# Attention without a row maximum, keys on partitions, under an order written by hand

## The chip, the cores and the metric

The kernel runs on one NeuronCore of one Trainium2 chip. The metric is the time of one execution on the device in microseconds; lower is better. The kernel before was timed three times: median 2095.51 us, from 2094.62 to 2095.75 us. All arithmetic is in float32.

## The reference, cut to what matters

Eight batches, twelve heads, 448 tokens and 64 dimensions a head; q and k are normalised by their root mean square over d, then softmax attention, and the result, 3584 rows of 768, goes through two matrix products with g = h - tanh(h) between them.

```python
q_n, k_n = (rmsnorm(q, g_q), rmsnorm(k, g_k))      # x / rms * g
scale = 1.0 / np.sqrt(q.shape[-1])
scores = scale * np.matmul(q_n, k_n.transpose(0, 1, 3, 2))
scores = scores - np.max(scores, axis=-1, keepdims=True)
attn = np.exp(scores)
attn = attn / (np.sum(attn, axis=-1, keepdims=True) + 1e-09)
attn_out = np.matmul(attn, v)                       # (8, 12, 448, 64) -> x: (3584, 768)
h = x @ w_in                                        # w_in: 768 x 2048
out = (h - np.tanh(h)) @ w_out                      # w_out: 2048 x 768
```

The inputs come from a fixed seed. g_q and g_k are |normal| + 0.5 in 64 entries each; drawn as the reference draws them, the largest product of the two is 5.26. The two weights reach the kernel as float64.

## The kernel before, in words

The work is 48 steps of attention, one for each batch and pair of heads, and eight batches of the two-layer MLP. 448 tokens lie on 112 partitions, four to a partition, so every token tile is a chunk c of 112.

`load` (L75) brings k, q and v of a step in, three DMAs on the queue of SyncE (SP). `prep` (L155) does the norm: GpSimd (POOL) squares 112x512 elements (L162), VectorE (DVE) sums them (L164) and adds the mean's terms (L165), POOL raises to the power -0.5 (L168), DVE multiplies (L169); four transposes on TensorE (PE, L176) turn the result so that (head, d) lies on partitions, and it is copied out of PSUM, for k with g_q * g_k * scale (L179), for q by ScalarE (ACT, L183). This happens for k and for q apart.

`attention` (L188) then takes each of four query chunks and two heads: a matmul gives scores with queries on partitions and keys free (L199), DVE finds the negated maximum of each row (L202), ACT does exp with that as its bias and sums the row on the way (L206), DVE turns the sum into a reciprocal (L210, L214), ACT multiplies the row by it (L215). Because the product with v has to contract over keys, every 112x112 block is transposed on PE (L223, 32 a step) and copied out of PSUM by DVE (L229) or ACT (L231); then the matmuls with v run (L233), two heads in the two halves of one PSUM tile. One copy puts the result into `xT` (L238), with tokens in their natural order.

`mlp_h` (L244) makes 128 hidden units of a batch: six matmuls of 448 columns (L252), tanh on ACT (L257), two subtractions on DVE (L260). `mlp_out` (L262) makes 128 tokens by 384 outputs: 16 matmuls (L268), an eviction (L274, L276), a store. In the trace every float32 matmul counts as two MATMUL instructions, a transpose as one.

`load_weight` (L113) turns a piece of a weight from the two words of each float64 into float32: four DVE instructions (L134, L141, L144, L147), three on POOL (L135, L138, L151) and one on ACT (L150), on 128x768 elements, 32 pieces in all. The loads go through ACT's queue (L124, L127).

The program text puts the attention of batch 0 with all weight pieces first, and then, for every batch, the attention of the next batch between its MLP units. What runs when on each engine isn't as written: the framework's scheduler orders the instructions by priority and by its own estimates of time, and picks free buffers. PSUM is split in three tiles for scores, two for transposes, one for the product with v and two for the MLP.

Of the kernel before, what the change touches and what calls it, by code (L numbers as in the profile page):

```python
# [9 lines left out]
F32 = mybir.dt.float32  # L10
I32 = mybir.dt.int32
U32 = mybir.dt.uint32
# [6 lines left out]
@with_exitstack  # L19
def kernel(  # L20
    ctx: ExitStack,
    tc: tile.TileContext,
    q: bass.AP,
    k: bass.AP,
    v: bass.AP,
    g_q: bass.AP,
    g_k: bass.AP,
    moe_w_in: bass.AP,
    moe_w_out: bass.AP,
    out: bass.AP,  # L30
):
    """Attention on pairs of heads, all in float32, one batch ahead of the MLP.

    Tokens of a batch lie on partitions as token = NCH * p + c, so that a load reads
    NCH whole rows per partition. A pair of heads gives 128 rows of x transposed,
    (head, d) on partitions and tokens free, which is what the MLP contracts over.
    """
# [3 lines left out]
    NT, DM = out.shape  # L41
    DFF = moe_w_out.shape[0]
    P = 128
    NCH = 4
# [7 lines left out]
    scale = 1.0 / float(D) ** 0.5  # L52
    assert 2 * D == P and NP == CD and 2 * REST == P and B % 2 == 0

    consts = ctx.enter_context(tc.tile_pool(name="consts", bufs=1))
# [30 lines left out]

    gcol = consts.tile([P, 2], F32, name="gcol")
    for base in (0, D):
        nc.scalar.dma_start(out=gcol[base : base + D, 0:1], in_=g_q[:, None])
        nc.scalar.dma_start(out=gcol[base : base + D, 1:2], in_=g_k[:, None])  # L90
    g_col = consts.tile([P, 1], F32, name="g_col")
    nc.vector.tensor_scalar(
        out=g_col, in0=gcol[:, 0:1], scalar1=gcol[:, 1:2], scalar2=scale, op0=ALU.mult, op1=ALU.mult
    )
    ident = consts.tile([P, P], F32, name="ident")
    make_identity(nc, ident)
    neg_half = consts.tile([CP, 2 * NCH], F32, name="neg_half")
    nc.vector.memset(neg_half, -0.5)

# [5 lines left out]
    w_in_words, w_out_words = (  # L105
        bass.AP(
            tensor=dataclasses.replace(w.tensor, shape=[w.shape[0], 2 * w.shape[1]], dtype=I32),
            offset=0, ap=[[2 * w.shape[1], w.shape[0]], [1, 2 * w.shape[1]]],
        )
        for w in (moe_w_in, moe_w_out)  # L110
    )

    def load_weight(pool, n):  # L113
        """A 128-wide piece of a weight, from the two words of its float64 to float32, rounded to nearest.

        2^20 + the upper mantissa bits + lo * 2^-32 is rounded once, to the float32 mantissa. Its power of
        two is the exponent field moved to float32's bias: 0 below its normal range, infinity above it.
        """
        f = n % CF
        raw = pool.tile([P, CD, P, 2], I32, name="w_raw")  # L120
        if n < CF:
            dst = w_in_sb[f].rearrange("p c f -> p (c f)")
            src = w_in_words[:, f * 2 * P : (f + 1) * 2 * P].rearrange("(c p) f -> p c f", p=P)
            nc.scalar.dma_start(out=raw.rearrange("p c f w -> p c (f w)"), in_=src)  # L124
        else:
            dst = w_out_sb[f]
            nc.scalar.dma_start(  # L127
                out=raw.rearrange("p c f w -> p (c f w)"), in_=w_out_words[f * P : (f + 1) * P, :]
            )
        lo, hi = (raw.rearrange("p c f w -> p (c f) w")[:, :, i] for i in range(2))  # L130
        ex = pool.tile([P, DM], I32, name="w_exp")
        man = pool.tile([P, DM], I32, name="w_man")
        exf, manf = ex.bitcast(F32), man.bitcast(F32)
# [208 lines left out]
```

## Time and profile before

| | value |
|---|---|
| median of three runs | 2095.51 us |
| span of the profiled execution | 2092.5 us |
| PE busy | 1931.4 us (92%), 6784 matmul instructions |
| DVE busy | 824.6 us (39%), 2142 instructions |
| ACT busy | 701.6 us (34%), 1581 instructions |
| POOL busy | 398.3 us (19%), 294 instructions |
| moved by DMA | 70.44 MB |

The profiled execution is known by its span, from its first instruction to its last; it lies 3.0 us under the median of the runs, which is what comes before and after the span. Busy time of PE is not PE at its best rate, because matmuls overlap and their ends are modelled. A row of the groups gives the line, the engine, what is written from what, the shape, the count, then the busy time in us, the mean of one in ns, the idle time of the engine ahead of it and who ended that. A row of the chain of waits gives a start, a duration and the work in it.

### The profile page before, as it was taken

How to read it: one execution, taken by the hardware profiler on the slowest of the kernel's cores; microseconds unless marked ns; L12 is line 12 of the kernel's file. 1: busy time of each engine (PE TensorE's matmuls, PEld its weight loads, DVE VectorE, ACT ScalarE, POOL GpSimd, SP SyncE). 2: the span in 40 equal slices, each digit the busy share in tenths (PEclk: the TensorE clock that was granted, in tenths of full speed). 3: DMA queues.
4: the chain of work that ended last, by engine and by line, in shares of the span. 5: the costliest groups of instructions: out<-in, count | busy, mean ns of one | idle time of the engine just before them, and what ended most of it. 6: DMA issues, size and time to landing. Idle time of an engine off the chain costs nothing. (4 is left out here: it accounts for less than half of the span.)

```text
span 2092.5 us, 19112 instructions
## 1 busy us (share of the span) xinstructions
PE 1931.4 (92%) x6784; PEld 938.5 (45%) x6784; DVE 824.6 (39%) x2142; ACT 701.6 (34%) x1581; POOL 398.3 (19%) x294
## 2 busy tenths in 40 slices
PE   4767689999999999999999999999999999999999
PEld 1322234454444544445444544445444554445555
DVE  6877764412543044432435025531455025430100
ACT  3344354412543034522445025530454024440100
POOL 5667642101221011111212012210122012100000
PEclk9766699999999999999999999999999999999999
DMA  4433310000000000000000000000000000000000
GB/s 113 128 104 127 119 42 27 19 25 25 22 23 26 19 21 27 22 26 24 22 23 23 24 25 23 27 22 19 27 23 27 20 24 18 5 2 22 0 12 19
DMA packets 58015, 70.44 MB, mean 34 GB/s; under 512 B 4160, under 2 KB 55872, under 8 KB 57920
## 3 DMA queue, kind: packets, MB, share of 16 engines
q1 hardware_dynamic: 42752, 44.05, 7.0%
q10 hardware_dynamic: 15168, 25.17, 3.8%
q8 instruction: 54, 0.88, 0.2%
q14 instruction: 41, 0.34, 0.0%
HBM read 58.20 MB, written 11.01 MB: 33 GB/s over the span
## 5 line engine op out<-in xcount | busy, mean ns | idle before, releaser
L252 PE MATMUL mm<-xT,w_in 128*128 128x448 f32 x1536 | 649.6, 549 | 1.9 <-DVE xT L238 1.9
L268 PE MATMUL mm<-w_out,gT 128*128 128x384 f32 x1536 | 504.9, 488 | 0.0
L268 PEld LDWEIGHTS mm<-w_out,gT 128*128 128x128 f32 x1536 | 289.0, 191 | 200.1 <-issue 9.9
L252 PEld LDWEIGHTS mm<-xT,w_in 128*128 128x128 f32 x1536 | 270.0, 195 | 210.4 <-issue 204.5
L223 PE MATMUL tp<-ident,attn 112*112 112x112 f32 x1536 | 254.0, 282 | 99.8 <-ACT attn L215 93.2
L223 PEld LDWEIGHTS tp<-ident,attn 112*112 112x112 f32 x1536 | 167.2, 138 | 372.0 <-ACT attn L215 229.8
L199 PE MATMUL sc<-kT,qT 64*112 64x448 f32 x768 | 284.7, 619 | 15.4 <-ACT attn L206 11.7
L162 POOL TENSOR_TENSOR n<-k_nat 112x512 f32<-112x512 f32 x48 | 52.4, 1091 | 1186.8 <-issue 1170.8
L215 ACT ACTIVATE attn<-attn,rden 112x448 f32<-112x448 f32 x384 | 238.6, 660 | 92.4 <-DVE rden L214 54.8
L206 ACT ACTIVATE attn<-sc,nmax 112x448 f32<-112x448 f32 x384 | 237.9, 623 | 81.7 <-DVE nmax L202 81.6
L233 PE MATMUL av<-attnT,v_nat 112*64 112x448 f32 x768 | 222.8, 586 | 13.7 <-DVE attnT L229 13.4
L202 DVE TENSOR_REDUCE nmax<-sc 112x1 f32<-112x448 f32 x384 | 225.1, 614 | 4.0 <-PE sc L199 2.6
L276 DVE COPY o_sb<-mm 128x384 f32<-128x384 f32 x28 | 15.6, 558 | 530.2 <-PE mm L268 530.2
L229 DVE COPY attnT<-tp 112x448 f32<-112x448 f32 x192 | 119.8, 624 | 257.8 <-PE tp L223 253.8
L231 ACT COPY attnT<-tp 112x448 f32<-112x448 f32 x192 | 101.9, 531 | 298.4 <-PE tp L223 284.4
L257 ACT ACTIVATE th<-mm 128x448 f32<-128x448 f32 x128 | 68.8, 538 | 300.6 <-PE mm L252 300.5
L274 ACT COPY o_sb<-mm 128x384 f32<-128x384 f32 x28 | 13.4, 480 | 463.6 <-PE mm L268 463.6
L199 PEld LDWEIGHTS sc<-kT,qT 64*112 64x112 f32 x768 | 93.9, 183 | 148.2 <-ACT attn L206 112.7
L260 DVE TENSOR_TENSOR gT<-mm,th 128x384 f32<-128x384 f32 x128 | 70.7, 553 | 150.2 <-ACT th L257 149.9
L233 PEld LDWEIGHTS av<-attnT,v_nat 112*64 112x64 f32 x768 | 49.0, 139 | 133.6 <-DVE attnT L229 103.8
L168 POOL TENSOR_TENSOR rr_q<-rr_q,neg_half 112x8 f32<-112x8 f32 x48 | 80.0, 1668 | 79.0 <-DVE rr_q L165 78.8
L168 POOL TENSOR_TENSOR rr_k<-rr_k,neg_half 112x8 f32<-112x8 f32 x48 | 80.9, 1684 | 66.6 <-DVE rr_k L165 66.1
(36 smaller groups left out, 1034.5 us busy)
## 6 DMA issues: line engine op xcount, KB each, us to landing
w_raw<-in_moe_w_in_dram ACTq DMA_DIRECT2D x16, 768.0 KB, 4.8
w_raw<-in_moe_w_out_dram ACTq DMA_DIRECT2D x16, 768.0 KB, 4.3
k_nat<-in_k_dram SPq DMA_DIRECT2D x48, 224.0 KB, 2.6
q_nat<-in_q_dram SPq DMA_DIRECT2D x48, 224.0 KB, 2.6
v_nat<-in_v_dram SPq DMA_DIRECT2D x48, 224.0 KB, 2.6
out_dram<-o_sb SPq DMA_DIRECT2D x48, 192.0 KB, 1.9
out_dram<-o_sb SPq DMA_DIRECT2D x16, 96.0 KB, 2.2
gcol<-in_g_q_dram ACTq DMA_DIRECT2D x2, 0.2 KB, 3.4
```

What stands on the lines that cost most here:

```text
L168: nc.gpsimd.tensor_tensor(out=rr, in0=rr, in1=neg_half, op=ALU.pow)
L199: nc.tensor.matmul(sc[:CP, :S], lhsT=qT[r, c * CP : (c + 1) * CP], rhs=kT[r, :], start=True, stop=True)
L202: nc.vector.tensor_reduce(out=nmax[:, h, c : c + 1], in_=sc[:CP, :S], op=ALU.max, axis=AX.X, negate=True)
L206: nc.scalar.activation(a, sc[:CP, :S], AF.Exp, bias=nmax[:, h, c : c + 1], scale=1.0, accum_out=den[:, h, c : c + 1],)
L215: nc.scalar.mul(a, a, rden[:, h, c : c + 1])
L223: nc.tensor.transpose(tp[:CP, c * CP : (c + 1) * CP], attn[h, c][:, kc * CP : (kc + 1) * CP], ident[:CP, :CP],)
L229: nc.vector.tensor_copy(out=aT[h], in_=tp[:CP, :S])
L231: nc.scalar.copy(out=aT[h], in_=tp[:CP, :S])
L233: nc.tensor.matmul(av[h * D : (h + 1) * D, :S], lhsT=v_nat[:, h, kc, :], rhs=aT[h], start=(kc == 0), stop=(kc == NCH - 1),)
L252: nc.tensor.matmul(hps[:, :S], lhsT=w_in_sb[f][:, c, :], rhs=xT[b, c], start=(c == 0), stop=(c == CD - 1),)
L260: nc.vector.tensor_tensor(out=dst, in0=hps[:, a:z], in1=th[:, a:z], op=ALU.subtract)
L268: nc.tensor.matmul(ops[:, :HALF], lhsT=g[:, f, :], rhs=w_out_sb[f][:, d], start=(f == 0), stop=(f == CF - 1),)
```

## The change

The kernel now has two paths and picks one at run time. It multiplies g_q and g_k, takes the largest square, compares it with (60 / (scale * 64))^2 = 7.5^2, reads the flag into a register, and branches. Where the flag is set, scores can't pass 60 in size and `bounded_path` runs; else `general_path`, which is the kernel before.

In `bounded_path`:

- The scores are made with keys on partitions and queries free, so that exp gives the operand for the product with v directly. The row maximum, the multiplication of each row and the 32 transposes of a step with their copies go. The 1e-9 goes too.
- k is turned without its norm; the norm of a key is the scale of exp, one value for each partition. One power instruction serves q and k together.
- The sum over keys is a matmul with a matrix of ones, of 64 columns for each head, beside the product with v. From batch 1 on, DVE first adds the four chunks of keys (`add`); in batch 0 the ones are multiplied with all four chunks. DVE takes the reciprocal of the 128x448 sums and multiplies the product with v by it.
- MLP: one subtraction of 448 columns in place of two; POOL copies the last 64 tokens for the shared tile.
- Weights are rounded in 64 half pieces. All loads, weights included, go through SP's queue.
- The order on each engine is the order of the program text (`manual_schedule`). `slot(s)` holds the work of attention for four neighbouring steps; between its parts stand four gaps, each of which issues a quarter of a slot's MLP matmuls, from slot 6 on. The 32 half pieces of w_in are spread over the gaps of slots -2 to 5, one a gap; those of w_out over the gaps of slots 6 to 8.

```diff
+    def norm(s):
+        rr = small.tile([CP, 2, 2 * NCH], F32, name="rr", bufs=3)
+        for i, name in enumerate("kq"):
+            rows = loaded[name, s].rearrange("p a b d -> p (a b) d")
+            sq = nat.tile([CP, 2 * NCH, D], F32, name="n", bufs=1)
+            nc.gpsimd.tensor_tensor(out=sq, in0=rows, in1=rows, op=ALU.mult)
+            nc.vector.reduce_sum(rr[:, i], sq, axis=AX.X)
+        rr2 = rr.rearrange("p i r -> p (i r)")
...
+        nc.gpsimd.tensor_tensor(out=rr2, in0=rr2, in1=neg_half, op=ALU.pow)
...
+    def scores(s, half):
+        rr, kT, qT = turned[s]
+        p = probs[s, half] = pp.tile([CP, 2, NCH // 2, S], F32, name="p")
+        for i in range(NCH // 2):
+            c = half * (NCH // 2) + i
+            tiles = []
+            for h in range(2):
+                r = slice(h * D, (h + 1) * D)
+                sc = ps_s.tile([P, 512], F32, name="sc")
+                nc.tensor.matmul(
+                    sc[:CP, :S], lhsT=kT[r, c * CP : (c + 1) * CP], rhs=qT[r, :], start=True, stop=True
+                )
+                tiles.append(sc)
+            for h in range(2):
+                nc.scalar.activation(
+                    p[:, h, i, :], tiles[h][:CP, :S], AF.Exp, scale=rr[:, 0, 2 * c + h : 2 * c + h + 1]
+                )
+
+    def add(s):
+        if s < NP:
+            sums[s] = []
+            return
+        t = sp.tile([CP, 2, S], F32, name="sum")
+        sums[s] = [t]
+        for h in range(2):
+            a, z = (probs[s, half][:, h].rearrange("p c q -> p (c q)") for half in range(2))
+            u = sp.tile([CP, 2 * S], F32, name="sum2")
+            nc.vector.tensor_tensor(out=u, in0=a, in1=z, op=ALU.add)
+            nc.vector.tensor_tensor(out=t[:, h, :], in0=u[:, :S], in1=u[:, S:], op=ALU.add)
+
+    def values(s):
...
+        for c in range(NCH):
+            p = probs[s, c // 2]
+            for h in range(2):
+                nc.tensor.matmul(
+                    av[h * D : (h + 1) * D, :S], lhsT=v_nat[:, h, c, :], rhs=p[:, h, c % 2, :],
+                    start=(c == 0), stop=(c == NCH - 1),
+                )
+        dn = ps_v.tile([P, 512], F32, name="dn")
+        t = sums.pop(s)
+        parts = t if t else [probs[s, c // 2][:, :, c % 2, :] for c in range(NCH)]
+        for i, p in enumerate(parts):
+            for h in range(2):
+                nc.tensor.matmul(
+                    dn[h * D : (h + 1) * D, :S], lhsT=ones[:CP, :D], rhs=p[:, h, :],
+                    start=(i == 0), stop=(i == len(parts) - 1),
+                )
+        rd = sp.tile([P, S], F32, name="rd")
+        nc.vector.reciprocal(rd, dn[:, :S])
+        x = xT[b, hp] = xp.tile([P, S], F32, name="xT")
+        nc.vector.tensor_tensor(
+            out=x.rearrange("r (p c) -> r c p", c=NCH), in0=av[:, :S].rearrange("r (c p) -> r c p", c=NCH),
+            in1=rd.rearrange("r (c p) -> r c p", c=NCH), op=ALU.mult,
+        )
...
+    def slot(s, gap):
...
+        if has(3):
+            load(s + 3, "kq")
+        if has(2):
+            norm(s + 2)
+        if has(1):
+            scores(s + 1, 0)
+        gap(0)
+        if has(0):
+            values(s)
+        if has(3):
+            load(s + 3, "v")
+        gap(1)
+        if has(1):
+            scores(s + 1, 1)
+            add(s + 1)
+        gap(2)
+        if has(2):
+            turn(s + 2)
+        gap(3)
...
+        for s in range(-2, NP + NP // 2):
+            def gap(j, s=s):
+                if s < NP:
+                    n = 2 * CF * (4 * (s + 2) + j + 1) // (4 * (NP + 2))
+                else:
+                    n = 2 * CF + 2 * CF * (4 * (s - NP) + j + 1) // (2 * NP)
+                    run(per_slot / 4)
+                weight(n + 3, n)
+            slot(s, gap)
...
+    bounded = nc.values_load(flag[0:1, 0:1])
+    with tc.If(bounded) as cmp:
+        with ExitStack() as arm, tc.manual_schedule():
+            bounded_path(tc, arm, q, k, v, moe_w_in, moe_w_out, out, g_col, ident, ones, neg_half)
+    with cmp.Else():
+        with ExitStack() as arm:
+            general_path(tc, arm, q, k, v, moe_w_in, moe_w_out, out, g_col, ident, neg_half)
```

`turn` makes the eight transposes of k and q with their two copies; `run` takes MLP matmuls from one stream, hidden units of a batch and then its outputs, batch after batch; `weight(n + 3, n)` loads half pieces up to n + 3 and rounds them up to n. PSUM is split in four tiles for scores and turns, one each for the product with v and for the sums, and two for the MLP.

331 lines of the change are left out of this document (266 added, 65 removed).

## Prediction

> **What bounds the kernel now.** I read the page first, its busy shares and its slices.
>
> ```profile
> span 2092.5 us, 19112 instructions
> PE 1931.4 (92%) x6784; PEld 938.5 (45%) x6784; DVE 824.6 (39%) x2142; ACT 701.6 (34%) x1581; POOL 398.3 (19%) x294
> ...
> PE   4767689999999999999999999999999999999999
> ...
> PEclk9766699999999999999999999999999999999999
> ```
>
> PE is full from the sixth slice on, at the full clock. Before that lies a stretch, the attention of batch 0 with the weights, in which PE is neither full nor at its clock. I took the end of that stretch from the writes of xT, and the shares in it from a table of windows.
>
> ```profile
> L238 DVE COPY xT<-av x6: 953/982/996, 61.5 to 262.9; 128x448 f32<-128x448 f32 x6
> ```
>
> ```profile
> core 0: us, PE busy (x) PEld busy (x) DVE busy (x) ACT busy (x) POOL busy (x), PEclk, DMA share, GB/s
> 0.00:265.00 265.00, 171.46 (x477) 68.21 (x478) 199.71 (x357) 101.14 (x209) 177.98 (x129) 0.75 0.38 118
> 600.00:1000.00 400.00, 386.69 (x1413) 192.95 (x1414) 134.55 (x386) 131.27 (x302) 47.76 (x36) 1.00 0.08 23
> ```
>
> The start takes 265 us. There DVE is busy 0.75 of the time and POOL 0.67, in turns: neither is full, yet together they set the pace. Afterwards DVE is at a third and PE sets it. What PE does there I price with the chain that ended last, where single bursts can be read (start, duration, work).
>
> ```profile
> 1782.57 0.90 PE av L233 x4
> 1783.47 0.91 PE tp L223 x8
> ...
> 1796.67 0.77 PE tp L176 x8
> 1797.44 0.99 PE sc L199 x4
> ...
> 1933.25 72.16 PE mm L252 x192
> 2005.41 82.57 PE mm L268 x256
> 2087.99 0.04 DVEq L276
> 2088.02 0.04 issue
> 2088.07 0.56 DVE o_sb L276
> ```
>
> The last three kinds show the MLP at PE's pace: 72.16 us for the hidden units of a batch, 82.57 for the outputs of four tiles. All of it is 8 x 72.16 + (1792 / 256) x 82.57 = 577.3 + 578.0 = 1155.3 us, or 24.07 for each of 48 steps. The other rows are attention: four matmul instructions of two heads take 0.90 (av) or 0.99 (sc), well under four times 72.16 / 192 = 0.38, so the two heads run side by side. 2092.5 - 265 - 1155.3 leaves 672 us for 42 steps of attention, 16.0 us each. By the rows it would be 4 x 0.90 + 4 x 0.91 + 0.77 + 4 x 0.99 = 12.0. The rest is in the groups of PE for that stretch:
>
> ```profile
> L199 PE MATMUL sc<-kT,qT 64*112 64x448 f32 x664 | 227.3, 578 | 7.5 <-ACT attn L206 4.5
> L223 PE MATMUL tp<-ident,attn 112*112 112x112 f32 x1344 | 207.8, 271 | 52.5 <-ACT attn L215 50.2
> ```
>
> Scores cost 227.3 / 42 = 5.4 a step, not 3.96, because many run without their partner; the transposes wait 52.5 us in all for ACT's division.
>
> **The change, part by part.** The durations on the other engines:
>
> ```profile
> L206 ACT ACTIVATE attn<-sc,nmax 112x448 f32<-112x448 f32 x384 | 237.9, 623 | 81.7 <-DVE nmax L202 81.6
> L229 DVE COPY attnT<-tp 112x448 f32<-112x448 f32 x192 | 119.8, 624 | 257.8 <-PE tp L223 253.8 <-PE av L233 3.3
> L168 POOL TENSOR_TENSOR rr_k<-rr_k,neg_half 112x8 f32<-112x8 f32 x48 | 80.9, 1684 | 66.6 <-DVE rr_k L165 66.1
> L260 DVE TENSOR_TENSOR gT<-mm,th 128x384 f32<-128x384 f32 x128 | 70.7, 553 | 150.2 <-ACT th L257 149.9 <-POOL w_out L151 0.3
> L214 DVE RECIPROCAL rden<-rden 112x1 f32<-112x1 f32 x384 | 56.9, 157 | 3.4
> L210 DVE TENSOR_SCALAR rden<-den 112x1 f32<-112x1 f32 x384 | 52.7, 146 | 49.4 <-ACT attn L206 48.8
> L162 POOL TENSOR_TENSOR n<-k_nat 112x512 f32<-112x512 f32 x48 | 52.4, 1091 | 1186.8 <-issue 1170.8 <-PE tp L176 13.5 <-DMA k_nat<-in_k_dram 2.4
> L147 DVE SCALAR_TENSOR_TENSOR w_man<-w_raw,w_man 128x768 f32<-128x768 uint32 x32 | 41.1, 1285 | 0.3
> L138 POOL TENSOR_SCALAR w_exp<-w_exp 128x768 int32<-128x768 f32 x32 | 39.4, 1232 | 2.7
> L141 DVE SCALAR_TENSOR_TENSOR w_exp<-w_raw,w_exp 128x768 int32<-128x768 int32 x32 | 38.9, 1214 | 15.9 <-POOL w_exp L138 15.8
> L135 POOL TENSOR_SCALAR w_exp<-w_exp 128x768 f32<-128x768 int32 x32 | 35.9, 1122 | 33.0 <-DVE w_exp L134 27.3 <-DVE rden L214 4.8
> L169 DVE TENSOR_TENSOR n<-k_nat,rr_k 112x512 f32<-112x512 f32 x48 | 34.5, 720 | 15.1 <-POOL rr_k L168 15.1
> L179 DVE TENSOR_SCALAR kT<-tp,g_col 128x448 f32<-128x448 f32 x48 | 32.6, 678 | 103.6 <-PE tp L176 103.6
> L164 DVE TENSOR_REDUCE rr_k<-n 112x8 f32<-112x512 f32 x48 | 32.6, 678 | 3.9 <-POOL n L162 3.8
> L151 POOL TENSOR_TENSOR w_in<-w_man,w_exp 128x768 f32<-128x768 f32 x16 | 29.3, 1833 | 17.0 <-ACT w_man L150 8.4 <-DVE w_exp L141 3.1 <-DVE rden L214 2.3
> L134 DVE TENSOR_SCALAR w_exp<-w_raw 128x768 int32<-128x768 int32 x32 | 28.5, 890 | 5.4 <-DMA w_raw<-in_moe_w_in_dram 5.4
> L144 DVE TENSOR_SCALAR w_man<-w_raw 128x768 int32<-128x768 int32 x32 | 20.3, 634 | 0.0
> ```
>
> *PE, steady slots.* Gone are the 32 transposes, 4 x 0.91 and their waits. Left are 16 score instructions, 4 x 0.99; 16 for the values, 4 x 0.90; 8 transposes, 0.77. Added are two matmuls with ones, four instructions of the same shape and pairing as av: 0.90. Sum 9.23 a step in place of 16.0, so a slot is 24.07 + 9.23 = 33.3 us. If scores ran as now (5.4), it would be 34.7; taken is 33.3, because both heads of a chunk stand side by side in the order and four score tiles are free when a burst of four matmuls begins.
>
> *ACT.* Eight exps of 0.62 us, 5.0 a slot, beside the tanhs; the division and the row sums go. They are hidden: the products of a slot use exps that stand at least three gaps of MLP work (18 us) before them. The other small edits cost nothing on PE's path. POOL's copy of the last tokens, 1024 elements, by L138 some 1232 / 768 x 1024 = 1.6 us, is read only after three tiles of outputs, 62 us later; if it came late, each of four odd batches would wait for it. k comes in two DMAs with pieces of 256 bytes, under a DMA share of 0.08 in the steady stretch and three slots ahead.
>
> *DVE.* The maxima and small operations go. The sums of keys are two additions of 896 and two of 448 elements; by L169 an addition of 512 takes at most 0.72, so 2 x (1.26 + 0.63) = 3.8 at most, taken 3.6. The product with the reciprocal is like the xT copy, 0.98, taken 1.0. The reciprocal of 448 elements in PSUM isn't in the trace. A copy of that size takes 0.62 (L229); on one element RECIPROCAL takes 157 - 146 = 11 ns longer than TENSOR_SCALAR, which at 448 elements would be 4.9. I take 4.0, nearer to the only row of this instruction. The Trainium skill, "VectorE: DVE Perf Modes", section "Walkthrough: the 8-slice pipeline in each mode", says that reciprocal iterates a divide with a repeat count of 8; an estimate from that page at 0.96 GHz is 448 x 8 / 0.96 = 3.7 us, and the sum below would fall by about 4 us; no run here shows it yet. In a steady slot DVE has then four reductions and multiplications (2 x 0.68 + 0.2 + 0.72 + 0.68 = 3.0), 4.0, 1.0, 3.6 and 2.67 subtractions of 0.65: 13.3 of 33.3 us, so it isn't the bound.
>
> *Waits behind the fixed order.* On DVE the reciprocal waits for the ones matmul, the sums for the exps; queued behind either are the MLP's subtractions, and PE waits for these through two PSUM tiles. A hidden tile takes PE 72.16 / 16 = 4.5 us, so a subtraction may come 4.5 us late. Reciprocal and product are 5.0 us, four exps and the sums 6.1, each followed by 0.65: 1.2 and 2.3 us over, at worst, in those slots that run hidden units (half of 42). At worst 21 x 3.5 = 74 us; taken 10, as a tile seldom ends just as the block begins. SP's queue now holds loads, weights and stores in one order; a step's loads stand two slots ahead of use, so a held store or weight costs nothing.
>
> *Start.* The branch needs the g rows landed and four small operations.
>
> ```profile
> gcol<-in_g_q_dram ACTq DMA_DIRECT2D x2, 0.2 KB, 3.4
> ```
>
> That is 3.4 us plus some 3 for issue and DVE. Reading the flag and jumping is in no row: from 0 to twice that landing with its issue, 10. First load at 6 to 16 us, taken 12. Then eight slots (-2 to 5), each with four half pieces. DVE: a half piece is (0.89 + 1.21 + 0.63 + 1.29) / 2 = 2.01, so 8.05, and attention 3.0 + 4.0 + 1.0 = 8.0; together 16.0. POOL: (1.12 + 1.23 + 1.83) / 2 x 4 = 8.4, two squares 2.2, one power of 16 values (1.7 if by instruction, 3.4 if by value, taken 2.5): 13.1. At the shares that these engines reach now in that mix, 16.0 / 0.75 = 21.4 and 13.1 / 0.67 = 19.6; 21.4 decides, 171 us for eight. Slots 6 to 8 hold 10.67 half pieces each: DVE 21.4 + 8.0 + 3.6 + 1.7 = 34.7, over 0.75 is 46.3, more than PE's 33.3; three are 139.
>
> *Sum.* 12 + 171 + 139 + 39 x 33.3 (1299) + the last batch's MLP 72.16 + 82.57 + 0.6 + 10 for the waits = 1786 us of span. The median of the runs lay 3.0 above the span before, so 1789.
>
> **The rivals.**
>
> *VectorE's queue holds PE.* The worst case above in full: 64 us more, 1853. For it: the order is strict, two PSUM tiles are few. Against: DVE is at 40%.
>
> *The reciprocal is as cheap as a copy.* Slots 0 to 8 are each (4.0 - 0.6) / 0.75 = 4.5 us shorter: 41 less, 1748. Against: the 11 ns.
>
> *The clock stays at half in the start.* The granted clock was 0.75 over the first 265 us, and 0.50 in one stretch of it:
>
> ```profile
> 68.00:78.00 10.00, 7.87 (x16) 3.27 (x16) 8.81 (x28) 7.37 (x17) 6.29 (x5) 0.50 0.25 79
> ```
>
> PE has per slot 9.23 and 12 further ones instructions (2.7), 11.9; at 0.50 of the clock throughout 23.9, over the 21.4 of DVE: 8 x 2.5 = 20 more, 1809. The Trainium skill, "TensorE: Matmul & The Clock Gate", Part 1, has only two rates, full and half, and a fall to half after about 3.4 us of idling, which speaks against sparse bursts in the start; the 0.75 here fits a mixture of the two.
>
> *Weights one at a time (slower).* All loads go through one queue in order, three raw buffers, and a half piece passes DVE, POOL, DVE, ACT, POOL. My sum gives (171 + 139) / 64 = 4.8 us a half piece. If each waits out its predecessor, it is a load of about 4.8 us
>
> ```profile
> w_raw<-in_moe_w_in_dram ACTq DMA_DIRECT2D x16, 768.0 KB, 4.8
> ```
>
> and 2.0 + 2.1 + 0.4 of work with handoffs of 0.5, 9.8: 12 + 64 x 9.8 + 1299 + 155 + 10 = 2103 of span, 2106. It gets slower than now from 9.6 us a half piece. Against: the same chain now passes 64 half pieces in 265 us, 4.1 each, beside six steps.
>
> *The other arm runs.* Then the time is the present one plus the start's 12, 2107. Against: the seeded g have a largest product of 5.26, under 7.5.
>
> **How the numbers follow.** The forecast has 0.65, with a range of its own from 1755 to 1830 (start at 6 to 16, the power at both ends, scores unpaired 39 x 1.4 = 55 in part). VectorE's queue 0.13, cheap reciprocal 0.09, half clock 0.08, weights 0.04, other arm 0.01. The range 1740 to 1865 holds all but the last two and the tails. No change is within 0.2%, what a measurement of this kernel can tell: 0.01 for a chance meeting. Slower 0.05, faster 0.94.
>
> **What would show it.** Right: no L223-like transposes; steady windows with PE full and about 33 us from one xT to the next; RECIPROCAL near 4 us; MLP matmuls from about 185 us, and slot 9 near 322. Wrong: xT spaced by 35 us or more in the late batches, with PE idle ended by DVE subtractions; POOL or DVE nearly full until 400 us; MLP matmuls that begin after 250 us.

## The result and the profile after

| | before | after |
|---|---|---|
| median of the runs | 2095.07 us (2094.14 to 2095.75, 4 runs) | 1762.43 us (1761.37 to 1764.9, 4 runs) |
| ratio to before, 95% interval | | 0.8411 [0.8399, 0.8423] |
| span of the profiled execution | 2092.5 us | 1759.5 us |

The forecast was 1789 us with a range of 1740 to 1865; the time is 26.6 us under it and inside the range. The profiled execution of after took 1761.65 us as a run, so 2.2 us lie around its span.

The page of after: the span, busy times, and the slices of PE and of its clock.

```profile
span 1759.5 us, 14368 instructions
...
PE 1621.6 (92%) x5512; PEld 804.2 (46%) x5512; DVE 705.2 (40%) x923; ACT 351.2 (20%) x653; POOL 388.9 (22%) x350
...
PE   1566767899999999999999999999999999999998
...
PEclk9776888999999999999999999999999999999999
```

PE has the same share, 92%, but 310 us less of work (1931.4 to 1621.6), and 1272 fewer matmul instructions. The picture is that of before: a start in which PE is neither full nor at its clock, then a long stretch at 9. Three windows of after and one more within its start give the stages (length, then busy time of each engine, granted clock, DMA share):

```profile
0.00:190.00 190.00, 91.73 (x368) 39.00 (x368) 115.73 (x186) 50.71 (x96) 107.94 (x122) 0.76 0.35 101
190.00:345.00 155.00, 121.19 (x349) 54.88 (x350) 114.89 (x180) 38.54 (x76) 85.53 (x105) 0.89 0.34 95
345.00:1605.00 1260.00, 1260.00 (x4365) 628.60 (x4365) 462.98 (x540) 251.90 (x463) 194.37 (x122) 1.00 0.10 27
```

```profile
63.00:180.00 117.00, 69.32 (x280) 28.20 (x280) 76.23 (x116) 34.06 (x65) 69.15 (x75) 0.72 0.33 97
```

In the steady stretch PE is busy 1260 of 1260 us at the full clock. PE waits for nothing there, so whatever a slot costs there is work of PE. What that work is, the chain that ended last shows in single bursts; one slot, from one product with v to the next:

```profile
804.16 3.16 PE av L228 x16
807.32 0.75 PE dn L237 x4
808.07 6.65 PE mm L286 x20
814.72 1.69 PE sc L199 x8
...
822.40 0.39 PE sc L177 x4
822.79 0.38 PE sc L182 x4
...
829.20 1.69 PE sc L199 x8
...
837.10 3.16 PE av L228 x16
```

Attention's bursts in a slot are 3.16 + 0.75 + 2 x 1.69 + 0.77 = 8.06 us. The first score bursts of slots 9 and 46 begin at 337.9 and 1549.5 us: 1211.6 for 37 slots, 32.75 each. Less the 24.07 of MLP that is 8.68, where a step of attention took 16.0 before; the 0.6 beyond the bursts lies at their seams.

The start is shorter too: the sixth xT, which ends the attention of batch 0, comes at 179.9 us, and before at 262.9. Those 83 us are a quarter of the gain, though after also puts off half of the rounding, that of w_out, to slots 6 to 8. Before slot 9, PE waits. Two stretches of after, by who ended PE's wait (us in total, times, longest):

```profile
PE sc L177 <- ACT p L204: 58.1, 7, 11.3
PE sc L199 <- DVE kT L179: 20.0, 7, 8.8
```

```profile
PE mm L259 <- DVE gT L266: 20.6, 6, 6.3
PE sc L199 <- DVE kT L179: 13.0, 4, 5.9
```

The first pair is from 0 to 190 us, in the start, where the transposes of `turn` come round to a score tile that exp has only just read. The second is from 190 to 345 us, slots 6 to 8: there the MLP's subtraction is late behind the rounding of w_out.

The groups of after for the operations whose cost was in doubt:

```profile
L204 ACT ACTIVATE p<-sc,rr 112x448 f32<-112x448 f32 x384 | 212.4, 633 | 382.7 <-PE sc L199 382.6
L242 DVE RECIPROCAL rd<-dn 128x448 f32<-128x448 f32 x48 | 141.9, 2955 | 249.6 <-PE dn L237 249.6
...
L218 DVE TENSOR_TENSOR sum<-p 112x896 f32<-112x896 f32 x84 | 91.7, 1092 | 151.9 <-ACT p L204 147.5
L161 POOL TENSOR_TENSOR rr<-rr,neg_half 112x16 f32<-112x16 f32 x48 | 139.3, 2902 | 50.7 <-DVE rr L160 49.6
```

And the end of its chain, the MLP of the last batch:

```profile
1598.96 72.16 PE mm L259 x192
1671.12 82.57 PE mm L286 x256
...
1753.77 0.56 DVE o_sb L296
```

### The profile page after: what moved, and what is told of

Same layout as the page of the kernel before. It is cut to its first block, busy times and chain, and to the rows that moved or that the text cites. A ratio compares the mean times of both kernels' runs of the same rounds, so it can differ in the third digit from the quotient of the medians.

```text
span 1759.5 us, 14368 instructions
## 1 busy us (share of the span) xinstructions
PE 1621.6 (92%) x5512; PEld 804.2 (46%) x5512; DVE 705.2 (40%) x923; ACT 351.2 (20%) x653; POOL 388.9 (22%) x350
## 4 chain that ended last, share of the span: by engine, by line
PE 80%; POOL 8%; DVE 8%; issue 2%; ACT 1%; DMA 0%; SPq 0%; POOLq 0%; ACTq 0%; DVEq 0%
PE mm L286 34%; PE mm L259 29%; PE sc L199 7%; PE av L228 7%; POOL w_exp L47 2%; POOL rr L161 2%; DVE w_exp L56 2%; POOL w_exp L44 2%; PE dn L237 2%; DVE rd L242 1%; POOL n L157 1%; DVE rr L158 1%; POOL w_out L60 1%; PE sc L177 1%; PE sc L182 1%
## 5 line engine op out<-in xcount | busy, mean ns | idle before, releaser
L259 PE MATMUL mm<-xT,w_in 128*128 128x448 f32 x1536 | 609.7, 551 | 20.7 <-DVE gT L266 20.6
L204 ACT ACTIVATE p<-sc,rr 112x448 f32<-112x448 f32 x384 | 212.4, 633 | 382.7 <-PE sc L199 382.6
L242 DVE RECIPROCAL rd<-dn 128x448 f32<-128x448 f32 x48 | 141.9, 2955 | 249.6 <-PE dn L237 249.6
L157 POOL TENSOR_TENSOR n<-k_nat 112x512 f32<-112x512 f32 x48 | 49.9, 1039 | 765.5 <-PE sc L182 758.2
L199 PE MATMUL sc<-qT,kT 64*112 64x448 f32 x768 | 183.6, 599 | 33.0 <-DVE kT L179 33.0
L228 PE MATMUL av<-p,v_nat 112*64 112x448 f32 x768 | 159.7, 559 | 0.0
L266 DVE TENSOR_TENSOR gT<-mm,th 128x448 f32<-128x448 f32 x128 | 79.5, 621 | 200.0 <-ACT th L265 200.0
L218 DVE TENSOR_TENSOR sum<-p 112x896 f32<-112x896 f32 x84 | 91.7, 1092 | 151.9 <-ACT p L204 147.5
L161 POOL TENSOR_TENSOR rr<-rr,neg_half 112x16 f32<-112x16 f32 x48 | 139.3, 2902 | 50.7 <-DVE rr L160 49.6
L199 PEld LDWEIGHTS sc<-qT,kT 64*112 64x112 f32 x768 | 66.6, 184 | 130.8 <-issue 91.6
L158 DVE TENSOR_REDUCE rr<-n 112x8 f32<-112x512 f32 x96 | 65.6, 683 | 92.9 <-POOL n L157 92.9
L164 DVE TENSOR_TENSOR n<-q_nat,rr 112x512 f32<-112x512 f32 x48 | 36.4, 759 | 147.0 <-POOL rr L161 147.0
L286 PE MATMUL mm<-w_out,g_rest 128*128 128x384 f32 x256 | 85.4, 489 | 0.0
L157 POOL TENSOR_TENSOR n<-q_nat 112x512 f32<-112x512 f32 x48 | 49.9, 1039 | 141.0 <-DVE rr L158 141.0
```

What stands on the lines that cost most here:

```text
L157: nc.gpsimd.tensor_tensor(out=sq, in0=rows, in1=rows, op=ALU.mult)
L158: nc.vector.reduce_sum(rr[:, i], sq, axis=AX.X)
L161: nc.gpsimd.tensor_tensor(out=rr2, in0=rr2, in1=neg_half, op=ALU.pow)
L199: nc.tensor.matmul(sc[:CP, :S], lhsT=kT[r, c * CP : (c + 1) * CP], rhs=qT[r, :], start=True, stop=True)
L204: nc.scalar.activation(p[:, h, i, :], tiles[h][:CP, :S], AF.Exp, scale=rr[:, 0, 2 * c + h : 2 * c + h + 1])
L218: nc.vector.tensor_tensor(out=u, in0=a, in1=z, op=ALU.add)
```

## The experiments

The theory (A, the prediction's) is that the steady slots are bound by PE alone, so that the gain there is the removed matmul work and the waits on the division, and that the start is set by VectorE and GpSimd taking turns. Rivals are that the order written by hand made the gain, that the removed maximum made it, or that VectorE's new work is close to binding everywhere. Every experiment is a version of after unless it says of before. "Slot" times are from the first score burst of one slot to that of the next.

**The order by hand.** The framework's scheduler orders the bounded path.

```diff
-        with ExitStack() as arm, tc.manual_schedule():
+        with ExitStack() as arm:
             bounded_path(tc, arm, q, k, v, moe_w_in, moe_w_out, out, g_col, ident, ones, neg_half)
```

> The new attention with the framework's own order in place of the hand-fixed one. Theory A (PE's instruction sum sets the steady slots): PE has 8.7 us of attention a step in either order, and only waits and unpaired scores come back, at most the 1.5 + 1.4 us a step that the kernel before had of them, 42 x 2.9 = 122 us: 1760 to 1885 us. Rival C (the order made the gain): most of the 333 us is lost, above 2000 us.

Measured: 1754.82 us (1754.17 to 1754.92), ratio to before 0.8363 [0.8349, 0.8377]. It is 7.6 us faster than after and lies below the range expected. Its steady slots take 32.7 us like those of after; slot 6 begins at 187.4 in place of 190.9, and slot 9 at 331.0 in place of 337.9, so all of the difference is made before slot 9. The gain does not come from fixing the order; here that costs a little. The text from which the scheduler starts is still the one written in slots, so what the order of the text brings by itself is not shown.

**The transposes.** From batch 1 on, 32 transposes a step are put back on PE, into a score tile, with nothing that reads them.

```diff
+        if s >= NP:
+            tx = ps_s.tile([P, 512], F32, name="sc")
+            for _ in range(8):
+                for c in range(NCH):
+                    nc.tensor.transpose(
+                        tx[:, c * CP : (c + 1) * CP], n[:, c].rearrange("p h d -> p (h d)"), ident[:CP, :CP]
+                    )
```

> The new kernel with 32 extra transposes of 112x112 in each step from batch 1 on, whose result nobody reads. Theory A: 32 x 0.096 us on PE in each of 42 slots, 3.1 us, 130 us more, about 1890 us. Rival: PE has room behind other waits and the transposes were costly only through their copies and waits: under 40 us more.

Measured: 1877.65 us (1877.05 to 1878.16), ratio 0.8954 [0.8936, 0.8971], 115.2 us over after. The chain of this kernel has the burst by itself:

```profile
796.14 3.07 PE sc L192 x32
```

The steady slots grew by that, to 35.8 us; 42 x 3.07 would be 129, and slots 4 to 8, which wait for other things, took up the rest. So a third of the 332.6 us gained is the bare PE time of the transposes, without the waits that they brought.

**The sums over keys.** All four chunks go through the ones matrix in every slot, and VectorE's additions go.

```diff
-        if s < NP:
+        if s < NS:
             sums[s] = []
             return
```

> All steps sum over keys on PE, four ones matmuls a head, and VectorE's four additions go. Theory A: six more pairs of matmul instructions at 0.376 us, 2.26 us in each of 42 slots, 95 us more, less up to 15 us in slots 6 to 8 where VectorE is relieved of 3.4 us each: 1842 to 1857 us. Rival B: VectorE's relief counts, 42 x 3.4 us less, faster than 1762 us.

Measured: 1839.43 us (1838.15 to 1840.88), ratio 0.8768 [0.8753, 0.8783], 77 us over after and just under the range expected. Its chain:

```profile
825.49 3.16 PE av L228 x16
828.65 3.01 PE dn L237 x16
```

The burst grew from 0.75 to 3.01 us and the slots from 32.75 to 35.0: PE's time passes into the end one to one, and 3.4 us of VectorE's work taken away (2 x 1.09 + 2 x 0.62) buys nothing there. Ahead of that it does: slot 9 begins at 326.1 us in place of 337.9.

**The heads apart.** In scores and values, all matmuls of one head stand before those of the other. This is the value part:

```diff
-        for c in range(NCH):
+        for h, c in [(h, c) for h in range(2) for c in range(NCH)]:
             p = probs[s, c // 2]
-            for h in range(2):
-                nc.tensor.matmul(
-                    av[h * D : (h + 1) * D, :S], lhsT=v_nat[:, h, c, :], rhs=p[:, h, c % 2, :],
+            nc.tensor.matmul(
+                av[h * D : (h + 1) * D, :S], lhsT=v_nat[:, h, c, :], rhs=p[:, h, c % 2, :],
```

> The matmuls of one head are issued ahead of those of the other in scores and values; the work is the same. Theory A with the pairing of neighbouring heads: 16 value instructions one after another are 15 x 0.376 = 5.6 us in place of 3.0, a half's eight score instructions 2.6 in place of 1.7, so 4.5 us a slot, 42 x 4.5 = 190 us more, about 1950 us. Rival: matmuls on different halves of the array run side by side wherever they stand in the queue: no change.

Measured: 1823.19 us (1821.85 to 1823.55), ratio 0.8691 [0.8676, 0.8705]. It is slower, as expected, but by 1.55 us a slot, a third of the 4.5 expected. The timeline of PE around one product with v:

```profile
790.95 3.65 PE L229 MATMUL av<-p,v_nat 112*64 112x448 f32 x13
794.07 0.59 PE L238 MATMUL dn<-sum,ones 112*64 112x448 f32 x1
794.43 0.54 PE L229 MATMUL av<-p,v_nat 112*64 112x448 f32 x1
...
794.81 0.92 PE L229 MATMUL av<-p,v_nat 112*64 112x448 f32 x2
```

In the text all 16 instructions of av stand before dn. The first of dn, for head 0, starts at 794.07, while three of av, for head 1, are still to start. If the queue holds them in the order of the text, a matmul for the free half of the array thus passes some that stand ahead of it. That fits the scores, with two chunks of each head, which lost nothing (their instructions still start in pairs 0.013 us apart), and the values, with four chunks of a head in a row, which lost all of it. The Trainium skill, "TensorE: Matmul & The Clock Gate", Part 3, section "The mechanism", says that matmuls keep program order in start and end, with no reordering; this trace of float32 matmuls on two halves does not agree, by the 0.74 us between 794.07 and 794.81.

**A second reciprocal.** The line with the reciprocal is there twice: 2.95 us more on VectorE in every slot.

```diff
         nc.vector.reciprocal(rd, dn[:, :S])
+        nc.vector.reciprocal(rd, dn[:, :S])
```

> The reciprocal of the sums is done twice, 2.96 us more on VectorE in each of 48 steps. Theory A: the steady slots have no PE wait and do not change; only slots 0 to 8, where VectorE and GpSimd set the pace, get 3 us longer each: 15 to 40 us more, 1777 to 1802 us. Rival B (VectorE's load sets the pace throughout): 48 x 2.96 = 142 us more, about 1905 us.

Measured: 1790.23 us (1789.62 to 1790.55), ratio 0.8533 [0.8518, 0.8547], 27.8 us over after. The steady slots stay at 32.7 us. Start slots take 26.4 in place of 23.4, and slots 6 to 8 48.8, 52.0 and 55.1 in place of 45.8, 49.0 and 52.1: each is longer by the whole of the added 3 us. VectorE's time costs nothing in the steady stretch and all of itself before slot 9.

**The old kernel without its maximum.** In before, the row maximum is left out (exp with a bias of 0); the division and the transposes stay.

```diff
-                nc.vector.tensor_reduce(
-                    out=nmax[:, h, c : c + 1], in_=sc[:CP, :S], op=ALU.max, axis=AX.X, negate=True
-                )
...
-                    a, sc[:CP, :S], AF.Exp, bias=nmax[:, h, c : c + 1], scale=1.0,
+                    a, sc[:CP, :S], AF.Exp, bias=0.0, scale=1.0,
```

> The kernel before without the row maximum: exp with a bias of zero (it leaves out the subtraction of the maximum). Theory A: PE's work is the same, so the steady steps lose only some of their waits, 1.5 us each at most, and the start loses 8 x 0.61 us of VectorE in six steps: 20 to 90 us less, 2005 to 2075 us. Rival B (the lighter VectorE made the gain): 225 us of it are gone, nearer to 1870 us.

Measured: 2280.15 us (2275.52 to 2282.54), ratio 1.0865 [1.0839, 1.0891]: slower than before by 185 us, though it does less. None of the expectations held. PE's waits from 315 to 2041 us, in before and in this kernel:

```profile
PE tp L223 <- ACT attn L215: 43.9, 75, 1.9
```

```profile
PE tp L219 <- ACT attn L211: 73.6, 39, 2.2
PE sc L198 <- ACT attn L202: 21.1, 37, 0.9
```

The same stretch as a window, and PE's timeline of this kernel around one of those waits:

```profile
315.00:2041.00 1726.00, 1629.38 (x5511) 793.43 (x5509) 433.66 (x1350) 541.72 (x1292) 205.58 (x156) 0.92 0.07 20
```

```profile
707.51 3.78 PE L198 MATMUL sc<-kT,qT 64*112 64x448 f32 x12
...
715.17 0.62 PE L219 MATMUL tp<-ident,attn 112*112 112x112 f32 x2 [2.16 <-ACT attn L211]
715.58 1.51 PE L264 MATMUL mm<-w_out,gT 128*128 128x384 f32 x2
```

Without the maximum the scheduler puts up to 12 score instructions of a step in a row, and PE then waits for exp and division, 2.16 us in one piece here. After that two MLP instructions take 1.51 us, where at the full clock it would be some 0.81 (0.32 from one to the next by 82.57 / 256, and the mean of 0.49 for the second): the granted clock has dropped. It is 0.92 over the window, where before had 1.00. The trace's record of the clock has only full and half: from 315 to 2041 us it stands at half in 36 stretches, 286.7 us together. PE was busy for 263.0 of these, which loses 131.5 us; the two waits grew by 48 (94.7 from 46.3, with 2.4 for the scores before), and the sixth xT came 12.6 later. That is 192, against 188 between the two spans (2280.8 and 2092.5). One fall of the clock, by windows ahead of it and behind it:

```profile
351.70:355.10 3.40, 1.19 (x3) 0.27 (x3) 1.74 (x6) 0.90 (x4) 2.21 (x2) 1.00 0.25 68
355.10:361.90 6.80, 6.38 (x12) 2.78 (x13) 1.27 (x8) 5.46 (x14) 0.00 (x0) 0.50 0.13 35
```

PE worked for 1.19 of the 3.40 us ahead of it; the rest are two waits, of 0.47 and 2.16 us. The Trainium skill, "TensorE: Matmul & The Clock Gate", Part 1, section "What's actually happening", lets the clock fall after at least one idle window of about 3.4 us; this trace does not agree, as the longest single wait in the stretch is 2.2 us. How little work makes the clock fall is not shown. Why the scheduler chose this order was not tried.

**The old kernel without maximum and division.** Before, with both left out: the transposes and their copies stay.

```diff
...
-                nc.vector.reciprocal(rden[:, h, c : c + 1], rden[:, h, c : c + 1])
-                nc.scalar.mul(a, a, rden[:, h, c : c + 1])
```

> The kernel before without the maximum and without the division by the row sum (both left out). Theory A: the transposes stay, and a step is at best 24.07 + 12.0 = 36.1 us, 42 of them 1516, with a start of 200 and a last batch of 155: about 1870 us, not under 1850. Rival B (ScalarE's and VectorE's work per score was the cost): as fast as the new kernel, 1760 us.

Measured: 2004.69 us (2004.0 to 2005.44), ratio 0.956 [0.9541, 0.9579]. Both expectations were too low. Taking the work of softmax away almost whole brings 90 us of the 333; a step in the middle batches still takes 38.1 us (40.1 before), and PE's wait has passed to the copies of the transposed blocks:

```profile
PE av L220 <- DVE attnT L216: 31.6, 35, 2.1
```

Of the 5.4 us a step that remain to after's 32.75, the transposes' own time is 3.07; the rest was not taken apart. The start was shorter by 20 us, with the sixth xT at 242.8 in place of 262.9; of the 83 us that after gains there, this leaves most to other parts of the change.

**Overlapped rounding.** VectorE's last step of a half piece and GpSimd's product are issued after the first steps of the next piece, with two buffers.

```diff
+    def finish():
+        nc.vector.scalar_tensor_tensor(
+            out=ex, in0=hi, scalar=-(2**31), in1=ex, op0=ALU.bitwise_and, op1=ALU.bitwise_or
+        )
+        nc.gpsimd.tensor_tensor(out=dst, in0=manf, in1=exf, op=ALU.mult)
...
+        later = round_weight(nc, wp, raws.pop(n), dst, HALF, deep=True)
+        weight_finish()
+        pending.append(later)
```

> The last two instructions of a half piece's rounding (VectorE's exponent step and GpSimd's product) stand behind the first steps of the next half piece, so that the two engines need not take turns. Theory A' (the start's slots are the length of a chain that passes from engine to engine, 3.7 us a half piece, not the busy time of either): a half piece falls towards VectorE's 2.4 us, slots -2 to 5 from 23.4 to 19 or 20 us, slots 6 to 8 by 7 to 10 each, 40 to 60 us less in all: 1700 to 1722 us. Rival: the two engines slow each other down when they run together, and the sum stays: within 10 us of 1762.

Measured: 1763.34 us (1762.05 to 1764.6), ratio 0.8406 [0.8389, 0.8423]: no gain, as the rival had it, with start slots of 23.3 us. The handoff inside a half piece isn't, by itself, what makes the start long.

**Overlapped rounding, three buffers.** The same with three buffers for the exponent, and the mantissa worked out in the weight's own place.

```diff
-    ex = pool.tile([128, n], I32, name="w_exp")
-    man = pool.tile([128, n], I32, name="w_man")
+    ex = pool.tile([128, n], I32, name="w_exp", **({"bufs": 3} if deep else {}))
+    man = dst.bitcast(I32) if deep else pool.tile([128, n], I32, name="w_man")
```

> As the run with overlapped rounding, but with three buffers of exponents, and the mantissas built in the weight's own place, so that no step of the next half piece waits for a buffer of the one before the last. Theory A'' (the overlap failed because each of two buffers was taken until GpSimd's last product): slots -2 to 5 fall by 2 us each, slots 6 to 8 by 5 to 6, 30 to 40 us less: 1722 to 1732 us. Rival A' is wrong (the two engines slow each other down): within 10 us of 1762. In both the steady slots stay at 32.7 us.

Measured: 1753.1 us (1752.8 to 1754.11), ratio 0.8357 [0.8343, 0.8371]: 9.3 us off after, a quarter of what was expected and within the 10 us of the rival. Start slots take 22.7 us. The same instruction on VectorE from 60 to 180 us, in after and in this kernel:

```profile
L56 DVE SCALAR_TENSOR_TENSOR w_exp<-w_raw,w_exp 128x384 int32<-128x384 int32 x21 | 11.7, 558 | 8.4 <-POOL w_exp L47 8.4
```

```profile
L54 DVE SCALAR_TENSOR_TENSOR w_exp<-w_raw,w_exp 128x384 int32<-128x384 int32 x21 | 17.9, 851 | 0.0
```

The wait of 8.4 us on GpSimd is gone and 6.2 of it came back as longer instructions. One of them, with what GpSimd did beside it:

```profile
88.02 0.69 POOL L42 TENSOR_SCALAR w_exp<-w_exp 128x384 int32<-128x384 f32 x1
88.26 0.85 DVE L54 SCALAR_TENSOR_TENSOR w_exp<-w_raw,w_exp 128x384 int32<-128x384 int32 x1
```

All 21 took 0.85 us: each began while GpSimd's conversion ran and ended about 0.40 us behind its end. In the reordered kernel below, one that began beside GpSimd's product (1.00 us) took 1.36 at 86.63 us and again ended 0.41 behind it, but one beside the power (2.97 us) took 0.55 at 82.23. So running the two engines at once gives less than their times apart would say, though not beside the power. The Trainium skill, "SBUF — State Buffer", section "SBUF: two separate sides", has VectorE and GpSimd share a pair of ports that one of them holds for a whole instruction while the other is blocked; the trace agrees for the conversion and the product, and not for the power.

Longer instructions are not all that holds this kernel. The chain of waits through a start slot now has a weight load in it, behind VectorE's postponed last step, which reads the raw buffer:

```profile
108.90 3.51 DMA w_raw<-in_moe_w_in_dram
```

**No branch.** The bounded path alone: no flag is read and the general path is left out, so the kernel serves only inputs under the bound. The two kernels after this one keep the branch and the general path.

> The changed kernel with the bounded path alone: no flag is read, no branch stands in the program, and the general path is left out of it. It holds only for inputs whose bound is met. (A) The branch costs what the first load shows, 4.09 us in place of 0.73: 3.4 us less, 1759 us. (B) Some of that lies beside other work of the start, since the slots of the start wait for weights and not for the first load: 0 to 1.5 us less, 1761 to 1762.5. (C) The branch was costed at 10 with the first load at 12; if reading the flag also delays other engines, which the first load doesn't show, it is 8 us less, 1754.

Measured: 1760.25 us (1759.44 to 1761.19), ratio 0.8395 [0.8384, 0.8407]; the interval overlaps that of after. The first load is at 0.73 us in place of 4.09 and slot 6 at 188.8 in place of 190.9, but slot 46 at 1549.2 in place of 1549.5. So 2.1 of the 3.4 us reach slot 6 and 0.3 the last slots. The spans differ by 1.8 us all the same; the other 1.5 lie behind the last copy of outputs, which ends 3.7 us ahead of the end in place of 5.2. It is 3.7 to 3.9 us in every kernel here without the branch and 5.2 to 5.5 in every one with it. The time falls between (A) and (B), but not for the reason of either; (C) is out.

**The start reordered.** The rounding of the kernel with three buffers; and in slots -2 to 8 ScalarE does the squares, rounding stands between squares, power and product with q, and the reciprocal stands behind a portion of rounding.

```diff
...
+        norm(s + 2, "a", nc.scalar)
+        if has(1):
+            scores(s + 1, 0)
+        weights()
+        norm(s + 2, "b")
+        weights()
+        norm(s + 2, "c")
+        mlp()
+        if has(0):
+            av, dn = values(s, divide_now=False)
+        weights()
+        if has(0):
+            divide(s, av, dn)
...
```

> On top of that, in slots -2 to 8 alone, the squares of q and k go to ScalarE, the power and the reciprocal are issued with rounding steps of other half pieces around them, and a half piece has five places in a slot in place of four. Theory A'': in the start the time is the order of two engines' queues, so filling GpSimd's 2.9 us power and VectorE's 2.96 us reciprocal with the other engine's work shortens slots -2 to 5 from 23.4 to 16 or 18 us and slots 6 to 8 from 49 to about 43: 60 to 85 us less than the new kernel, 1677 to 1702 us. Rival (loads or the half clock of PE set the start): not under 1722 us, and the slots of the start not under 21 us.

Measured: 1718.2 us (1716.39 to 1718.53), ratio 0.8188 [0.8174, 0.8202]: 44 us faster than after, above the range expected. Start slots take 18.5 us, slot 6 begins at 154.2. The reason shows in one start slot of after, by GpSimd and then by VectorE:

```profile
97.03 1.04 POOL L157 TENSOR_TENSOR n<-k_nat 112x512 f32<-112x512 f32 x1
98.86 1.04 POOL L157 TENSOR_TENSOR n<-q_nat 112x512 f32<-112x512 f32 x1 [0.80 <-DVE rr L158]
100.91 2.91 POOL L161 TENSOR_TENSOR rr<-rr,neg_half 112x16 f32<-112x16 f32 x1 [1.01 <-DVE rr L160]
...
110.94 0.54 POOL L44 TENSOR_SCALAR w_exp<-w_exp 128x384 f32<-128x384 int32 x1 [2.98 <-DVE w_exp L43]
```

```profile
103.85 0.69 DVE L164 TENSOR_TENSOR n<-q_nat,rr 112x512 f32<-112x512 f32 x1 [3.02 <-POOL rr L161]
...
106.73 2.95 DVE L242 RECIPROCAL rd<-dn 128x448 f32<-128x448 f32 x1
109.71 0.95 DVE L244 TENSOR_TENSOR xT<-av,rd 128x448 f32<-128x448 f32 x1
```

During the power VectorE stands idle for 3.02 us, and during reciprocal and product GpSimd for 2.98, because in this order nothing of the next half piece stands there for them. The chain of waits through this slot, from 93.3 to 116.7 us, passes over GpSimd and VectorE alone, with no piece of PE or of a load, so neither rival sets it. With rounding placed in these gaps, and the two squares (2 x 1.04 us) moved from GpSimd to ScalarE, a slot is 4.9 us shorter than in after and 4.2 than with three buffers alone. How much of that the placing brings and how much the squares is not shown. Slots 6 to 8 took 44.0, 49.9 and 46.8, hardly less than in after; the reordered kernel waits there for the subtraction (165 to 310 us):

```profile
PE mm L290 <- DVE gT L297: 29.3, 6, 8.2
```

**Rounding in twelfths.** The reordered kernel, with the rounding of slots 6 to 8 one half piece at a time behind each twelfth of the MLP work, and ScalarE's step issued with `finish`.

```diff
     def finish():
+        nc.scalar.mul(manf, manf, 2.0**-20)
...
-                    run(per_slot / 4)
+                    for _ in range(3):
+                        run(per_slot / 12)
+                        weight_part(True)
```

> The kernel of the reordered start with two edits. In slots 6 to 8 the half pieces of w_out come one at a time behind each twelfth of the slot's MLP matmuls, in place of two or three together; and the multiplication on ScalarE is issued one half piece late, with the last two steps, so that it no longer waits there for VectorE ahead of a tanh. Reordered start: 1718.2 us, slots 6 to 8 together 140.7 us, of which PE was busy 115.7 of 145 between 165 and 310 us and waited 29.3 for the subtraction's gT. (A) These slots are long because the tanh and the subtraction stand behind a bunch of rounding in their queues: they fall to 115 to 128 us together, the time to 1693 to 1706 us, and PE's waits on gT to under 12. (B) They are long because VectorE and GpSimd have that much to do there, slowed by each other: the same instructions in finer portions take as long, slots 6 to 8 stay at 136 to 146 us and the time at 1713 to 1723.

Measured: 1704.16 us (1703.4 to 1705.36), ratio 0.8128 [0.8116, 0.8141], the fastest of all and 58 us under after. Slots 6 to 8 take 39.3, 43.4 and 46.1, together 128.8 in place of 140.7; another 3.2 us were gained before slot 6 (at 150.9 in place of 154.2), where only the late step on ScalarE is new. The waits for the subtraction, from 165 to 310 us again, are down, though not under 12:

```profile
PE mm L290 <- DVE gT L297: 18.1, 6, 6.2
```

(B) is out. (A) holds for the time, but the slots stay just above its range: the two edits together took 12 of the 43 us by which these slots exceeded PE's own 98. What is left was not taken apart by a run. The window from 150 to 290 us has VectorE busy 0.88 of the time and the clock at 0.93, so here the work of VectorE itself comes near, and the chain of waits through the three slots holds four weight loads, 13 us together.

## Why the prediction was right, and where its terms were off

**What bounds it.** Right: PE, in full, from slot 9 on. The rival by which VectorE's queue holds PE is shown wrong for that stretch by the window with 1260 of 1260 and by the second reciprocal, which left the slots at 32.7. The 10 us of waits were 0 there. The place where that rival does act is slots 6 to 8, with 20.6 us.

**Steady slot.** 33.3 us forecast, 32.75 measured. Single terms: the product with v 3.16 (3.60 forecast), scores 3.38 (3.96), ones 0.75 (0.90), transposes 0.77. The matmuls of two heads go in pairs every 0.37 to 0.38 us once a burst runs; bursts of four, from which the prices came, contain the ends, which long bursts pay once. That is 20 us of the sum's excess over 37 slots.

**Tail.** 155.3 forecast behind the last slot. The MLP of the last batch took the same 72.16 and 82.57, but the sum held half a tile of outputs twice: 42 slots of 24.07 us already contain 1010.9 of the MLP's 1155.3 us, which leaves 144.4 for the tail and not 154.7. From the start of slot 46 to the end it was 210.0 us, where the forecast had 66.6 + 155.3 = 221.9: 10.3 for the half tile, 4.9 for the scores and transposes that the last two slots don't have, 1.1 for their pace, less 4.6 for the last store, which the 0.6 behind the copy left out (5.2 us lie between the end of that copy and the end of the span, 1.5 of them with the branch).

**First load.** 12 us forecast (6 to 16), 4.1 measured, below the range. The g rows and the four operations were done at 3.4 us, where the sum had 6.4, and reading the flag and jumping took 0.7 more, where it had some 5.6 by no row at all. By the kernel without it, the branch costs 3.4 us in the first load, of which 0.3 last to slot 46, and 1.5 behind the last copy.

**Start slots.** 21.4 us forecast, 23.4 measured: eight slots 186.8 us from the first load to slot 6, against 171. VectorE's work was 76.23 / 5 = 15.2 us a slot (16.0 forecast), but its share was 76.23 / 117 = 0.65 and not the 0.75 carried over from before. That share is the term that was mis-sized: it was carried over from another kernel's order. A free scheduler does not bring it back by itself: under it slots 0 to 5 take 23.6 us on average, 24.1 in after. The reordered kernel does 15.4 us of VectorE's work in 18.5 us, a share of 0.83, with two squares less on GpSimd. The rival of the half clock is out for these slots: the clock granted over the first 190 us was 0.76, and the chain of waits through a start slot has no piece of PE.

**Slots 6 to 8.** 139 us forecast, 147.0 measured. Here the share held: VectorE was busy for 108.4 of the 147.0 us, 0.74. Its work was larger, 36.1 us a slot in place of 34.7.

**Single prices.** The reciprocal took 2.955 us, inside 0.62 to 4.9, under the 4.0 taken: the difference of 11 ns on one element was over one and a half times the price of an element in a long row. 448 elements in 2.955 us is at most 6.6 ns each. The estimate from the Trainium skill, "VectorE: DVE Perf Modes", section "Walkthrough: the 8-slice pipeline in each mode", 3.7 us, is nearer than 4.0 and still 25% over; the measurement decides. The power of 16 values took 2.90 us (2.5 taken, 1.7 to 3.4), so most of it goes by value: 8 values took 1.68, the other 8 took 1.22 more. Sums took 3.4 us (3.6), the product 0.96 (1.0).

**The sum.** 7.9 us too little before slot 6 (7.9 too much for the first load, 15.8 too little for the slots), 8.0 too little in slots 6 to 8; from slot 9 to the end 1421.6 us measured, where the forecast had 1299 + 155.3 + 10, so 42.7 too much (20 of pace, 10 of waits, 12 behind slot 46). Together 26.8 too much, and the span is 26.5 under the forecast's 1786. So the total is nearer than its parts: start and steady stretch erred in opposite ways, and that they nearly met is luck.

**The other rivals.** The general path did not run. Rounding weights one after the other took 186.8 us for 32 half pieces with their slots, 5.8 each, below the 9.6 from which it would have been slower than before. The reciprocal was not as cheap as a copy.

## What to carry to other kernels

Price a stretch by its bounding engine and long bursts there, and ask in each stretch anew which engine that is: the same 3 us on VectorE cost nothing from slot 9 on and all of itself before. When an order is fixed by hand, a long instruction on one of two engines that work in turns needs other work placed behind it for its partner, and a short evacuation that a matmul waits for must not stand behind a bunch of filler. Where a scheduler sets the order, leaving an operation out also changes the order, so a removal is priced only in the order that will run.

## What the runs showed of the hardware

- A float32 matmul that uses half of the array's columns started 0.74 us ahead of others that stand before it in the text and use the other half.
- A reciprocal of 448 elements took 2.955 us, 4.7 times a copy of 448 elements (0.62); a power on GpSimd took about 0.15 us more for each value on a partition (1.68 for 8, 2.90 for 16).
- The same rounding instruction on VectorE took 0.56 us with GpSimd waiting, 0.85 where it began within a conversion of 0.69 us on GpSimd, 1.36 beside a product of 1.00, and 0.55 beside a power of 2.97.
- From 315 to 2041 us of a kernel whose longest wait on PE there was 2.2 us, the granted clock stood at half in 36 stretches, 287 us together. Ahead of one of them PE had worked for 1.19 of 3.40 us.
